# Gated mix of two attentions on one core: the first block of x loaded ahead of the first weights, which come and are cast in two halves

## The chip, the core and the metric

The kernel runs on one NeuronCore of a Trainium2 chip. The metric is the time of one execution on the device, in microseconds (us). The core has five engines that run their own instruction streams and wait for each other with semaphores: TensorE (PE; its weight loads are listed apart as PEld), VectorE (DVE), ScalarE (ACT), GpSimd (POOL) and SyncE (SP), which here issues all DMA transfers. Data come from the chip's memory (DRAM) into on-chip tiles of 128 partitions, and TensorE writes its products into PSUM banks.

## The reference

One token sequence x of 2048 tokens by 448 features goes through two attention layers of 16 heads with 28 features each, and a gate of each token mixes their outputs.

```python
g = sigmoid((x * gate_w).sum(-1, keepdims=True))
# A: linear attention; features of q and k by a small matrix of each head and two softmaxes
pq, pk = q_A @ w_phi, k_A @ w_phi
phi_q = concat(softmax(pq), softmax(-pq));  phi_k = concat(softmax(pk), softmax(-pk))
a = ((phi_q @ (phi_k.T @ v_A)) / (phi_q @ phi_k.sum(0) + 1e-6)) @ A_wo
# B: full softmax attention
b = (softmax(q_B @ k_B.T * 28 ** -0.5) @ v_B) @ B_wo
out = g * a + (1 - g) * b
```

q, k and v of each layer are x times that layer's wqkv. All inputs and the output are float32.

## The kernel before, in words

**Precision.** TensorE is fast on a rounded 32-bit type (fp32r). A float32 matrix is therefore split into a high part, its cast to fp32r, and a low part, what the cast left out. A product of two such matrices is three products: high by high, high of x by low of w, low of x by high of w. XH and XL hold the high and low parts of x, wB those of B's weights for q and k.

**Tiling.** The 448 features are four blocks b of 128 partitions; the last block holds 64 rows twice, so that its upper half can take the low part of x there (L718). The tokens are cut into four columns t of 512. Layer B's q and k come out as seven row blocks m of 128 by 512 tokens, a unit (m, t) being one PSUM bank: 11 products for a unit (3 for each of the blocks 0 to 2, 2 for the block 3).

**The start.** `first_units` (L696 to L732) makes the units m = 0 to 3 of t = 0 side by side, in four banks, while its data arrive. For each block b, SP issues two loads of 256 KB: the first 512 columns of the weights (L701) and 512 tokens of x (L702), both into the two halves of one buffer `raw[b]`. Buffers 0 to 2 are from the pool `stg`, of three; buffer 3 is from the pool `ev`. `x_loads(1)` (L703, issued at L141) asks for the next 512 tokens, into the same three buffers of `stg`, so these loads wait until a buffer has been read. Then come eight products of the identity with itself (L707, L708) into the fourth bank. Nothing reads them, and the first useful product there starts the bank anew. They are float32, which TensorE runs as two records each. The identity is made by GpSimd at the very start (masks.py:197 and 199).

For each block the casts follow: ScalarE casts the weights (L711), VectorE casts x for block 0 and ScalarE for the others (L712), VectorE subtracts for the low parts of the weights (L713) and of x (L715, L718). TensorE's products (L725) are written in this order for blocks 0 to 2: the four m with high by high, the four m with the low part of the weights, the four m with the low part of x. For block 3 it goes by m. That makes 44 products. A load of the weights of a product (PEld) stands ahead of each.

**After it.** Units 4 to 19 of B's q and k (`proj_qk`, L118) use the next x; then layer A's keys, values and queries with feature maps, B's values, and a first pass over B's scores that takes maxima (L296, L337, L348). From about 330 us on, the scores of B are computed again (L1040), go through the exponential on ScalarE (L1043) and meet the values (L1144), group by group; the two outputs are projected and mixed at the end.

**What sets the order.** The order on TensorE, VectorE, ScalarE and GpSimd is that of the program text. SP is not in that list: the framework's scheduler orders the DMA issues on it. DMAs tell of their landing by eight semaphores that are taken in turn.

The change touches `first_units` alone.

Of the kernel before, what the change touches and what calls it, by code (L numbers as in the profile page):

```python
# [17 lines left out]
P = 128  # L18
# [17 lines left out]
def f32(ap):  # L36
    return ap.bitcast(F32)
# [3 lines left out]
def gated_mix_kernel(ctx, tc, xT, wqkB, wvB, wvA, wkAT, wqAT, phi, woA, woB,  # L41
# [7 lines left out]
    nc = tc.nc  # L49
# [14 lines left out]
    def ps_s(nm):  # L64
        if turn4:
            turn4.append(nm)
            if len(turn4) % 4 == 0:
                return ps_pv(nm)
        return ps.tile([P, 512], F32, tag="s", name=nm, bufs=psn[0])

    def ps_pv(nm):
        return ps.tile([P, 512], F32, tag="pv", name=nm, bufs=1)

    def ps_mx(nm, d):
        return ps.tile([P, 2, 512], F32, tag="md" if d and psn[1] == 3 else "mx", name=nm,
                       bufs=1 if d and psn[1] == 3 else 2)
# [582 lines left out]
    def keep_qk(m, t, pq, ev):  # L659
        tt = slice(t * 512, (t + 1) * 512)  # L660
        e = ev.tile([P, 2, 512], F32R, tag="ev", name=f"ev{t}_{m}")
        nc.scalar.copy(e[:, 0, :], pq)  # L662
        nc.vector.tensor_sub(e[:, 1, :], pq, f32(e[:, 0, :]))  # L663
        nc.sync.dma_start(qk_d[m * P:(m + 1) * P, :, tt], f32(e))
# [14 lines left out]
    def x_loads(t):  # L679
        loads(("x", t), lambda: load_x(t, 0), lambda: load_x(t, 2))  # L680
# [7 lines left out]
    def splits(n):  # L688

        if n % 4 == 1 and n < 12:  # L690
            split_x(n // 4 + 1, raws.pop(("x", n // 4 + 1)))
        if n in (14, 15):
            split_part(wB[1], "wB1", 384, n - 14)
        take_lows()

    def first_units():  # L696

        raw = [stg.tile([P, 2, 512], F32, tag="stg", name=f"first_raw{b}") for b in range(3)]
        raw.append(f32(ev.tile([P, 2, 512], F32R, tag="ev", name="first_raw3")))
        for b in range(4):  # L700
            nc.sync.dma_start(raw[b][:, 0, :], wqkB[:, b, :512])  # L701
            nc.sync.dma_start(raw[b][:, 1, :], xT[:, b, :512])  # L702
        x_loads(1)  # L703
        pqs = [ps_s(f"pqk0_{m}") for m in range(3)] + [ps_pv("pqk0_3")]
        pr = [ps_mx(f"pqk_{i}", False) for i in range(2)]
        later.extend((pr[0][:, 0, :], pr[1][:, 0, :]))
        for _ in range(8):  # L707
            nc.tensor.matmul(pqs[3][:, :P], ident, ident, start=True, stop=True)  # L708
        for b in range(4):
            w, x = wB[0][:, :, b, :], XH[:, b, :512]  # L710
            nc.scalar.copy(w[:, 0, :], raw[b][:, 0, :])  # L711
            (nc.scalar.copy if b else nc.vector.tensor_copy)(x, raw[b][:, 1, :])  # L712
            nc.vector.tensor_sub(w[:, 1, :], raw[b][:, 0, :], f32(w[:, 0, :]))  # L713
            if b < 3:
                nc.vector.tensor_sub(XL[:, b, :512], raw[b][:, 1, :], f32(x))  # L715
                todo = [(0, x), (1, x), (0, XL[:, b, :512])]
            else:
                nc.vector.tensor_sub(x[64:], raw[b][64:, 1, :], f32(x[64:]))  # L718
                todo = [(0, x), (1, x)]
            if b < 3:  # L720
                order = [(i, m) for i in range(3) for m in range(4)]
            else:
                order = [(i, m) for m in range(4) for i in range(2)]
            for i, m in order:
                nc.tensor.matmul(pqs[m], w[:, todo[i][0], m * P:(m + 1) * P], todo[i][1],  # L725
                                 start=b == 0 and i == 0, stop=b == 3 and i == 1,
                                 skip_group_check=True)
        hold = raws[("x", 1)][0][:1, 0, :4]
        splits(1)
        nc.gpsimd.tensor_copy(phi_s[:1, :, 0], hold)  # L730
        for m in range(4):
            keep_qk(m, 0, pqs[m], ev)  # L732

    later = []
    first_units()
    pkv = ps_pv("pkv")
    for n in range(4, NP):
# [637 lines left out]
```

## Time and profile before

| what | us |
|---|---|
| median of 3 runs (1001.2 to 1002.0) | 1001.29 |
| the profiled execution, its time | 1001.51 |
| its span, first to last instruction | 999.7 |
| TensorE busy | 991.4 |
| ScalarE busy | 807.4 |
| VectorE busy | 666.3 |
| GpSimd busy | 231.7 |
| mean granted TensorE clock | 0.999 |

The profile is of one execution. Its times count from the first instruction, and the execution's own time is 1.8 us longer than the span. A timeline row reads: start in us, length in us, engine, line of the kernel, operation, output tile <- input tile, shapes, count (x8 means that eight neighbours were merged, and the length is that of all), and in brackets the time that the engine stood idle before it and what ended that. SPq rows are the issues of DMAs: the length is the issue's own, and the data land later. A line of the chain of waits gives start, length and what the end of the program was waiting for at that time. Records of TensorE products overlap: a new one starts before the one ahead of it has ended, so the distance of starts is what a product costs.

### The profile page before, as it was taken

How to read it: one execution, taken by the hardware profiler on the slowest of the kernel's cores; microseconds unless marked ns; L12 is line 12 of the kernel's file. 1: busy time of each engine (PE TensorE's matmuls, PEld its weight loads, DVE VectorE, ACT ScalarE, POOL GpSimd, SP SyncE). 2: the span in 40 equal slices, each digit the busy share in tenths (PEclk: the TensorE clock that was granted, in tenths of full speed). 3: DMA queues.
4: the chain of work that ended last, by engine and by line, in shares of the span. 5: the costliest groups of instructions: out<-in, count | busy, mean ns of one | idle time of the engine just before them, and what ended most of it. 6: DMA issues, size and time to landing. Idle time of an engine off the chain costs nothing.

```text
span 999.7 us, 18087 instructions
## 1 busy us (share of the span) xinstructions
PE 991.4 (99%) x6456; PEld 553.5 (55%) x6456; DVE 666.3 (67%) x1343; ACT 807.4 (81%) x1532; POOL 231.7 (23%) x214
## 2 busy tenths in 40 slices
PE   9999999999999999999999999999999999999998
PEld 8878878887777533333333333333334444455656
DVE  6567666888764588878888788888886544444202
ACT  5445555568855899999999999999999999979672
POOL 1265455668415111110120100102001011101010
PEclk9999999999999999999999999999999999999999
DMA  8976312412445732332524324443233354216231
GB/s 291 316 243 211 121 59 78 169 46 79 119 131 133 163 96 56 78 79 64 114 58 108 81 51 142 90 99 94 59 90 77 76 113 120 51 37 148 62 106 56
DMA packets 69170, 109.09 MB, mean 109 GB/s; under 512 B 18216, under 2 KB 29112, under 8 KB 69080
## 3 DMA queue, kind: packets, MB, share of 16 engines
q1 hardware_dynamic: 69080, 107.94, 40.0%
q8 instruction: 51, 0.84, 0.4%
q14 instruction: 39, 0.32, 0.1%
HBM read 74.33 MB, written 31.45 MB: 106 GB/s over the span
## 4 chain that ended last, share of the span: by engine, by line
PE 95%; DMA 2%; SPq 1%; DVE 1%; issue 1%; ACT 0%; POOL 0%; POOLq 0%; DVEq 0%; ACTq 0%
PE st L1040 28%; PE pv L1144 25%; PE pm L337 9%; PE pqk L118 6%; PE pva L136 4%; PE pk L136 4%; PE pq L118 4%; PE pob L118 3%; PE pvb L136 2%; PE poa L118 2%; PE pmb L296 2%; PE pft L558 1%; PE pqk L725 1%; PE pkv L512 1%; DMA oTa<-oTa 1%; PE poL L1182 1%
## 5 line engine op out<-in xcount | busy, mean ns | idle before, releaser
L1043 ACT ACTIVATE p<-st 128x512 f32<-128x512 f32 x1020 | 527.2, 638 | 25.9 <-PE st L1040 25.9
L348 DVE TENSOR_REDUCE part<-pm 128x1 f32<-128x512 f32 x450 | 287.3, 685 | 150.5 <-PE pm L337 150.5
L1040 PE MATMUL st<-qst,kst 128*128 128x512 f32 x1020 | 301.0, 423 | 0.4 <-DVE acc L1159 0.4
L1144 PE MATMUL pv<-p,vb 128*32 128x512 f32 x2048 | 263.7, 602 | 0.0
L1040 PEld LDWEIGHTS st<-qst,kst 128*128 128x128 f32 x1020 | 168.7, 187 | 99.6 <-ACT p L1043 45.0
L341 ACT ACTIVATE rl<-pm 128x512 f32<-128x512 f32 x200 | 124.3, 622 | 13.9 <-PE pm L337 12.4
L337 PEld LDWEIGHTS pm<-kc,qc 28*128 28x128 f32 x800 | 38.2, 181 | 167.7 <-issue 101.4
L441 POOL TENSOR_TENSOR oUb<-oUb,rsb 128x512 f32<-128x512 f32 x15 | 19.3, 1288 | 460.9 <-DMA rsb<-rdb 299.1
L345 DVE CUSTOM_DVE_ANT_0 rl<-pm,rl 128x512 f32<-128x512 f32 x150 | 102.0, 680 | 0.0
L337 PE MATMUL pm<-kc,qc 28*128 28x512 f32 x800 | 101.3, 495 | 0.0
L1144 PEld LDWEIGHTS pv<-p,vb 128*32 128x32 f32 x2048 | 47.3, 108 | 95.6 <-issue 89.5
L305 DVE CUSTOM_DVE_ANT_0 rl<-pmb,rl 128x512 f32<-128x512 f32 x112 | 72.0, 680 | 34.9 <-ACT rl L303 34.8
L303 ACT ACTIVATE rl<-pmd 128x1024 f32<-128x1024 f32 x56 | 57.5, 1027 | 17.9 <-issue 8.7
L118 PE MATMUL pqk<-XH,wB 128*128 128x512 f32 x192 | 59.3, 397 | 0.0
L662 ACT CAST ev<-pqk 128x512 fp32r<-128x512 f32 x28 | 16.0, 589 | 36.6 <-PE pqk L118 25.2
L118 PE MATMUL poa<-woA_s,oTa 128*128 128x448 f32 x128 | 38.0, 378 | 2.8 <-DMA oTa<-oTa 2.4
L118 PEld LDWEIGHTS pqk<-XH,wB 128*128 128x128 f32 x192 | 35.4, 188 | 8.5 <-issue 1.5
L1159 DVE SCALAR_TENSOR_TENSOR acc<-pob,gate,acc 128x448 f32<-128x448 f32 x12 | 8.2, 680 | 47.3 <-PE pob L118 47.3
L136 PE MATMUL pva<-wvA_s,XH 128*128 128x450 f32 x128 | 38.6, 375 | 0.0
L136 PE MATMUL pk<-wkA_s,XH 128*128 128x448 f32 x128 | 37.5, 374 | 0.0
L118 PE MATMUL pq<-wqA_s,XH 128*128 128x448 f32 x128 | 37.3, 374 | 0.0
L663 DVE TENSOR_TENSOR ev<-pqk,ev 128x512 fp32r<-128x512 f32 x28 | 19.0, 689 | 27.0 <-ACT ev L662 24.3
(169 smaller groups left out, 1172.6 us busy)
## 6 DMA issues: line engine op xcount, KB each, us to landing
qkd<-ev SPq DMA_DIRECT2D x28, 512.0 KB
qst<-qkd SPq DMA_DIRECT2D x64, 224.0 KB
kst<-qkd SPq DMA_DIRECT2D x64, 224.0 KB
od<-oTb SPq DMA_DIRECT2D x48, 112.0 KB
rsa<-rda SPq DMA_DIRECT2D x32, 128.0 KB
rsb<-rdb SPq DMA_DIRECT2D x15, 256.0 KB
kc<-qkd SPq DMA_DIRECT2D x64, 56.0 KB
gad<-ga SPq DMA_DIRECT2D x16, 224.0 KB
```

What stands on the lines that cost most here:

```text
L118: nc.tensor.matmul(d, l, r, start=i == 0, stop=i == len(todo) - 1)
L136: nc.tensor.matmul(dst[:, :n], l, r, start=i == 0, stop=i == len(todo) - 1, skip_group_check=True)
L296: nc.tensor.matmul((pb if j < 2 else pd)[:, j % 2, :], qc[js, qt * P:(qt + 1) * P], kc[js, :], start=True, stop=True, tile_position=(32 * ...
L303: nc.scalar.activation(rl, pd, AF.Relu)
L305: nc.vector.tensor_tensor_reduce(rl[:, i, :], pb[:, i, :], rl[:, i, :], 1.0, LOWEST, ALU.add, ALU.max, part[:, col + i:col + i + 1])
L337: nc.tensor.matmul(pm[j], mxs[("qc", gq)][js, qt * P:(qt + 1) * P], mxs[("kc", g, kb)][js, :], start=True, stop=True, tile_position=(32 * ...
L341: nc.scalar.activation(rl, pm[kb], AF.Relu if kb < 3 else AF.Copy)
L345: nc.vector.tensor_tensor_reduce(r, pm[j], r, 1.0, LOWEST, ALU.add, ALU.max, part[:, col + j:col + j + 1])
L348: nc.vector.tensor_reduce(part[:, col + j:col + j + 1], pm[j], AX.X, ALU.max)
L1040: nc.tensor.matmul(st, kst_of[(gq // NQ, kt // 4)][:, j, (kt % 4) * P:(kt % 4 + 1) * P], qst_of[gq][:, j, :], start=True, stop=True)
L1043: nc.scalar.activation(p, st, AF.Exp, scale=SCALE)
L1144: nc.tensor.matmul(pv[32 * j:32 * j + 32, :], vb[kt // 8][:, kt % 8, 4 * g + j, :], pt[j], start=kt == 0, stop=kt == NT - 1, tile_position ...
```

## The change

Four things change in `first_units`. The load of x's block 0 is issued first. The weights of block 0 come behind it as two loads of 256 columns each, and ScalarE casts them in two instructions of 256 columns. The blocks 1 to 3 keep their loads and casts. The banks of the four units are claimed at the top. Two of the eight warming products no longer use the identity: VectorE clears 128x128 elements of buffer 3, in the place that the fourth block's weights take later, and two products run on that; six run on the identity as before, behind the statements that issue the loads.

```diff
         raw.append(f32(ev.tile([P, 2, 512], F32R, tag="ev", name="first_raw3")))
-        for b in range(4):
+        pqs = [ps_s(f"pqk0_{m}") for m in range(3)] + [ps_pv("pqk0_3")]
+        a = raw[3][:, 0, :P]
+        nc.vector.memset(a, 0.0)
+        for _ in range(2):
+            nc.tensor.matmul(pqs[3][:, :P], a, a, start=True, stop=True)
+        nc.sync.dma_start(raw[0][:, 1, :], xT[:, 0, :512])
+        for c in (0, 256):
+            nc.sync.dma_start(raw[0][:, 0, c:c + 256], wqkB[:, 0, c:c + 256])
+        for b in range(1, 4):
             nc.sync.dma_start(raw[b][:, 0, :], wqkB[:, b, :512])
             nc.sync.dma_start(raw[b][:, 1, :], xT[:, b, :512])
         x_loads(1)
-        pqs = [ps_s(f"pqk0_{m}") for m in range(3)] + [ps_pv("pqk0_3")]
         pr = [ps_mx(f"pqk_{i}", False) for i in range(2)]
         later.extend((pr[0][:, 0, :], pr[1][:, 0, :]))
-        for _ in range(8):
+        for _ in range(6):
             nc.tensor.matmul(pqs[3][:, :P], ident, ident, start=True, stop=True)
         for b in range(4):
             w, x = wB[0][:, :, b, :], XH[:, b, :512]
-            nc.scalar.copy(w[:, 0, :], raw[b][:, 0, :])
+            for c in range(0, 512, 512 if b else 256):
+                cs = slice(c, c + (512 if b else 256))
+                nc.scalar.copy(w[:, 0, cs], raw[b][:, 0, cs])
             (nc.scalar.copy if b else nc.vector.tensor_copy)(x, raw[b][:, 1, :])
             nc.vector.tensor_sub(w[:, 1, :], raw[b][:, 0, :], f32(w[:, 0, :]))
```

## The prediction

> **What bounds the kernel now.** I read the page's busy shares first, then its chain of work that ended last.
>
> ```profile
> PE 991.4 (99%) x6456; PEld 553.5 (55%) x6456; DVE 666.3 (67%) x1343; ACT 807.4 (81%) x1532; POOL 231.7 (23%) x214
> PE 95%; DMA 2%; SPq 1%; DVE 1%; issue 1%; ACT 0%; POOL 0%; POOLq 0%; DVEq 0%; ACTq 0%
> ```
>
> TensorE works for 991.4 of 999.7 us, so whatever brings its useful work forward can be kept to the end, and only that. Next the first pieces of the chain in order of time, since the change touches nothing behind 15 us.
>
> ```profile
> 1.36 3.68 PE pqk L708 x16
> 5.04 10.04 PE pqk L725 x44
> 15.08 22.44 PE pqk L118 x99
> ```
>
> The columns are start, length, what. Warming products run to 5.04, then 44 useful ones at 10.04 / 44 = 0.228 us each, without a hole. So the term to find is how far the 44 move as a row, and which of them waits for data after the change. For that, the timeline of the first 8 us.
>
> ```profile
> 0.74 0.39 SPq L701 DMA_DIRECT2D first_raw<-in_wqkB_dram  x1
> 0.81 0.09 DVE L172 MEMSET red<- 128x32 f32 x1 [0.81 <-PEq L1362]
> 1.01 0.29 POOL masks.py:199 TENSOR_SCALAR_AFFINE_SELECT ident<-ident 128x128 f32<-128x128 f32 x1
> 1.19 0.41 SPq L702 DMA_DIRECT2D first_raw<-in_xT_dram  x1
> ...
> 1.36 3.68 PE L708 MATMUL pqk<-ident 128*128 128x128 f32 x16 [1.36 <-POOL ident masks.py:199]
> 1.65 0.43 SPq L701 DMA_DIRECT2D first_raw<-in_wqkB_dram  x1
> 2.12 0.43 SPq L702 DMA_DIRECT2D first_raw<-in_xT_dram  x1
> ...
> 3.54 0.43 SPq L701 DMA_DIRECT2D first_raw<-in_wqkB_dram  x1
> 3.63 0.62 ACT L711 CAST wB<-first_raw 128x512 fp32r<-128x512 f32 x1 [1.61 <-DMA first_raw<-in_wqkB_dram]
> ...
> 4.28 0.43 DVE L712 CAST XH<-first_raw 128x512 fp32r<-128x512 f32 x1 [3.39 <-DMA first_raw<-in_xT_dram]
> 4.63 0.68 DVE L713 TENSOR_TENSOR wB<-first_raw,wB 128x512 fp32r<-128x512 f32 x1
> 4.83 1.67 PEld L725 LDWEIGHTS pqk<-XH,wB 128*128 128x128 f32 x8
> 4.86 2.06 PE L725 MATMUL pqk<-XH,wB 128*128 128x512 f32 x8
> 5.23 0.68 DVE L715 TENSOR_TENSOR XL<-first_raw,XH 128x512 fp32r<-128x512 f32 x1
> 5.96 0.62 ACT L711 CAST wB<-first_raw 128x512 fp32r<-128x512 f32 x1 [1.71 <-DMA first_raw<-in_wqkB_dram]
> ...
> 6.64 0.62 ACT L712 CAST XH<-first_raw 128x512 fp32r<-128x512 f32 x1
> ```
>
> The first useful weight load stands at 4.83: the last input, x's cast, ends at 4.28 + 0.43 = 4.71, and 0.12 us later TensorE goes. That 0.12 is my hand-over below. But a second thing ends there as well:
>
> ```profile
> 4.51 0.33 PEld L708 LDWEIGHTS pqk<-ident 128*128 128x128 f32 x1
> ```
>
> The last warming load runs from 4.51 to 4.84. Data and warming train end together, and moving one alone brings nothing.
>
> **The change, part by part.** *Warming train.* Today it waits for the identity (GpSimd, 1.01 + 0.29 = 1.30) and starts at 1.36, 0.06 later. The new first two products need a 128x128 clear on VectorE behind the 0.09 us one at 0.81. No row shows that clear on VectorE: not below 0.09 (a quarter of the columns), not above the 0.29 of the identity's GpSimd step; I take 0.2, nearer the upper since it is the same shape. 0.90 + 0.2 + 0.06 = 1.16, so the train starts and ends about 0.18 us earlier (bounds 0.10 to 0.31). VectorE pays nothing: it idles 3.39 us before 4.28. The length stays eight products.
>
> *x first.* x takes the slot of 0.74 on SP and lands as the weights did, by 3.63; cast on VectorE 3.63 to 4.06, 0.65 earlier than now. Every later load of the queue moves one slot back, since the halves are one issue more: 1.65 to 2.12, that is 0.47. The fourth weight block's load now also waits for two warming products that read its buffer; they are done at about 2.1 (1.16 and a quarter of the train's 3.68), that load comes at 3.54 + 0.47 = 4.01, so nothing queued behind it on SP (the last x block and the x loads of L141) is held.
>
> *Weights in halves.* The rate of the transfers:
>
> ```profile
> 2.50:3.63 1.13, 1.13 (x7) 1.13 (x6) 0.00 (x0) 0.00 (x1) 0.00 (x0) 1.00 1.02 386
> 3.63:4.28 0.65, 0.65 (x5) 0.65 (x4) 0.00 (x0) 0.62 (x1) 0.00 (x0) 1.00 1.15 337
> 4.28:5.96 1.68, 1.68 (x10) 1.51 (x9) 1.63 (x3) 0.01 (x1) 0.00 (x0) 1.00 0.92 276
> ```
>
> The last two columns are the busy share of the DMA engines and GB/s. They are full from 2.5 us on, and 256 KB at 386 GB/s is 0.68, which agrees with 4.28 - 3.63 = 0.65 between the first two landings. So a transfer costs its bytes and the earlier issue of a later one hides: 0.47 of issue is less than 0.65 of transfer. At best the halves land at 3.96 and 4.28. At worst each costs what a whole block does, 0.65: 4.28 and 4.93. I take the bytes, with up to 0.1 more for twice the rows. The Trainium skill's page DMA: Bandwidth & Descriptors (Anatomy of one DMA) gives each transfer some 2 us fixed plus its bytes, which taken as a serial price would put the second half 2 us later; the 0.65 between two landings here says that this share overlaps.
>
> The cast of a half on ScalarE has a row in the tail of the kernel:
>
> ```profile
> L1243 ACT CAST oTlast<-oUlast x2: 403/404/406, 989.8 to 990.1; 128x256 fp32r<-128x256 f32 x2
> ```
>
> First half 3.96 + 0.40 = 4.36, hand-over to 4.48: data is ready 0.35 earlier than 4.83. The train is not: with 0.18 it lets the useful row go at 4.65. Second half 4.28 + 0.40 = 4.68, needed by the third product at about 5.1: covered.
>
> *Where the stall goes.* The fifth product needs the low part of the weights, and VectorE takes it from the whole 512 columns.
>
> ```profile
> 5.63 0.19 PEld L725 LDWEIGHTS pqk<-XH,wB 128*128 128x128 f32 x1
> ```
>
> Today the low part is done at 4.63 + 0.68 = 5.31, and its load at 5.63 waits for nothing. After: 4.68 + 0.03 + 0.68 = 5.39, with the hand-over 5.51, while TensorE wants it at 5.63 - 0.18 = 5.45. It waits 0.06, or 0.16 if the halves cost 0.1 more. Of 0.18, 0.02 to 0.12 is left.
>
> Then comes the second block. Its weights land at 5.96, its x is cast by 6.64 + 0.62 = 7.26.
>
> ```profile
> 7.44 1.77 PEld L725 LDWEIGHTS pqk<-XH,wB 128*128 128x128 f32 x8
> ```
>
> TensorE wants it at 7.44; with the hand-over it is there at 7.38. So at most 0.06 of the gain passes this point, as long as that block lands when it does now; with 0.1 more for the halves it is 0.04 of loss. Behind it there is cover:
>
> ```profile
> 8.26 0.62 ACT L712 CAST XH<-first_raw 128x512 fp32r<-128x512 f32 x1
> 10.16 1.77 PEld L725 LDWEIGHTS pqk<-XH,wB 128*128 128x128 f32 x8
> 12.40 1.05 ACT L377 CAST XH<-xraw 128x1024 fp32r<-128x1024 f32 x1 [0.45 <-DMA xraw<-in_xT_dram]
> 14.70 0.41 PEld L118 LDWEIGHTS pqk<-XH,wB 128*128 128x128 f32 x2
> ```
>
> The third block is cast at 8.88 and wanted at 10.16, the next x at 13.45 against 14.70. A delay of under 1.2 us is lost in there.
>
> **Sum.** Between -0.06 and +0.04 us; I take -0.05. The profiled execution took 1001.51 us, of which the span is 999.7 and 1.8 lie around it: it becomes 1001.46. It stood 0.22 above the median of the three runs, 1001.29, which therefore becomes **1001.2 us**: no change that a measurement tells. A measurement of this kernel can tell about 0.2%, 2 us, from no change; the three runs alone spread over 0.8 us.
>
> **Rivals.** *The gain is kept.* For it: landings 0.65 apart would put the second block's weights at 4.93 and not at 5.96; the 276 GB/s row shows that they were slowed, perhaps by chance. Then the second block binds nothing and 0.12 to 0.18 remain: 1001.1. Against it: it needs an accident to go away.
>
> *The extra transfer holds the second block.* If issue and not bytes set its landing, it comes 0.47 later, cast by 7.73, wanted at 7.44, there at 7.85: +0.4; with each half as dear as a whole block, 7.26 + 0.65 + 0.12 = 8.03, +0.6. 1001.7 to 1001.9. Against it: the full DMA engines from 2.5 us on.
>
> *The clock comes late.* Warming is for the TensorE clock:
>
> ```profile
> 1.36:4.86 3.50, 3.50 (x17) 3.50 (x17) 0.58 (x2) 1.27 (x2) 0.84 (x1) 1.00 0.76 242
> L708 PEld LDWEIGHTS pqk<-ident x16: 288/333/333, 1.4 to 4.5; 128*128 128x128 f32 x16
> L558 PEld LDWEIGHTS pft<-ident,feat x128: 137/140/143, 190.0 to 264.1; 128*128 128x128 f32 x128
> ```
>
> The clock column says 1.00 for the train, but the same load of 128x128 takes 333 ns there and 140 ns later: the train ran at about half speed, and the first useful load at 4.83 takes 0.19 as all later ones do. So the clock doubled near 4.8, about 3.4 us after TensorE began. I count on it to move with the train. If it does not, each us of delay makes TensorE do half of what it could: half of the delay is lost, at most half of another 3.4, 1.7 us: up to 1003.0, if the doubling fell one such stretch later. The Trainium skill's page TensorE: Matmul & The Clock Gate (Part 1) says just this, that the window of 3413 ns runs free and does not start with the kernel. The 3.4 us here agree with its length; one trace can't show its phase, and by that rule the kernel before has the same lottery.
>
> *The order on SP flips, and it is slower.* Only the four compute engines have their order written by hand; SP's is made by the scheduler:
>
> ```profile
> 11.54 0.42 SPq L749 DMA_DIRECT2D sel_s<-in_sel_dram  x1
> 13.24 2.10 SPq L141 DMA_DIRECT2D xraw<-in_xT_dram  x2
> ```
>
> L749 is written at unit 14 and goes ahead of x loads written at unit 5. One more DMA at the head could change an order later. The place where that costs is the stretch where TensorE waits for a chain of DMAs:
>
> ```profile
> 279.75 3.57 DMA oTa<-oTa
> ...
> 300.71 3.55 DMA oTa<-oTa
> ```
>
> One issue slipped behind such a landing costs 3.6 us: 1004.9. It decides from the point where an issue of these chains stands behind one that it precedes now. Against it: the plan shifts as a whole, by less than one slot of 0.47 us. The same slip the other way would save up to 3.6: 997.7.
>
> **How the numbers follow.** Forecast 0.50; gain kept 0.13; second block held 0.17; late clock 0.10; SP order slower 0.06, faster 0.04. Faster by over 0.2% (under 999.3) is the last alone, 0.04; slower (over 1003.3) the one before, 0.06; within 0.2%: 0.90. The range takes in the first three cases, 0.80, the runs' own spread, and a late clock of up to half its price: 1000.5 to 1002.4.
>
> **What the profile after would show.** The train from about 1.16; the first useful load at about 4.65 (at 4.5 if the train is not what holds it, at 4.8 if the halves land late); a short hole ahead of the fifth product, with VectorE's low part named; the second block's first load at 7.38 to 7.48; from 15 us on the same picture, shifted by less than 0.1. Wrong it would be if that second load stands past 7.8, if useful products ahead of some later point are 0.45 us apart (the clock), or if the stretch from 255 to 304 us changes its length.

## The result, and the profile after

The changed kernel takes 1003.48 us (median of 10 runs, 1001.37 to 1005.51), the kernel before 1001.60 in the runs beside it (10 runs, 1001.2 to 1002.1). The ratio is 1.0018, with a 95% interval of 1.0009 to 1.0026. That is a loss of 1.9 us where 0.05 of gain was forecast, and the time lies above the forecast's range of 1000.5 to 1002.4. The profiled execution of after took 1005.02 us with a span of 1003.2, 3.5 more than that of before.

The page's busy shares and its chain by engine:

```profile
PE 993.7 (99%) x6456; PEld 555.6 (55%) x6456; DVE 666.8 (66%) x1344; ACT 806.9 (80%) x1533; POOL 232.5 (23%) x214
PE 88%; DMA 6%; SPq 2%; DVE 2%; POOL 1%; issue 1%; ACT 1%; POOLq 0%; ACTq 0%; DVEq 0%
```

TensorE is as full as before, but its share of the chain fell from 95% to 88%, and DMA took up 4 of the 7 points. So somewhere DMAs now set the end. First the start of the kernel, from the timeline of after:

```profile
0.74 0.40 SPq L705 DMA_DIRECT2D first_raw<-in_xT_dram  x1
...
1.09 1.22 PE L704 MATMUL pqk<-first_raw 128*128 128x128 f32 x4 [1.09 <-DVE first_raw L702]
...
3.67 0.43 DVE L721 CAST XH<-first_raw 128x512 fp32r<-128x512 f32 x1 [2.64 <-DMA first_raw<-in_xT_dram]
...
3.99 0.40 ACT L720 CAST wB<-first_raw 128x256 fp32r<-128x256 f32 x1 [1.98 <-DMA first_raw<-in_wqkB_dram]
4.53 1.20 PE L734 MATMUL pqk<-XH,wB 128*128 128x512 f32 x2
...
5.61 0.41 ACT L720 CAST wB<-first_raw 128x256 fp32r<-128x256 f32 x1 [1.21 <-DMA first_raw<-in_wqkB_dram]
6.04 0.69 DVE L722 TENSOR_TENSOR wB<-first_raw,wB 128x512 fp32r<-128x512 f32 x1 [1.94 <-ACT wB L720]
6.06 1.94 PE L734 MATMUL pqk<-XH,wB 128*128 128x512 f32 x6 [0.33 <-ACT wB L720]
...
7.12 0.62 ACT L720 CAST wB<-first_raw 128x512 fp32r<-128x512 f32 x1 [1.10 <-DMA first_raw<-in_wqkB_dram]
7.41 3.41 SPq L141 DMA_DIRECT2D xraw<-in_xT_dram  x3
```

Everything up to the first useful product went as planned: it starts at 4.53, 0.33 ahead of before. Then the **second half of the weights** is cast only at 5.61, when ScalarE had idled 1.21 us for its DMA; the first half was cast at 3.99, so the halves landed 1.6 us apart. TensorE has two products to do meanwhile, which fill 1.20 us at the half clock of the start, and it still idles 0.33. Block 1's weights come at 7.12 instead of 5.96, and the first load of the next x (L141), which waits for buffer 0 to be read, is issued at 7.41 instead of 5.98, where before has it:

```profile
5.98 0.39 SPq L141 DMA_DIRECT2D xraw<-in_xT_dram  x1
```

What DMA did in that time, in windows of 0.5 us (the last three columns are granted clock, busy share of the DMA engines and GB/s). Before:

```profile
3.50:4.00 0.50, 0.50 (x4) 0.50 (x4) 0.00 (x0) 0.37 (x1) 0.00 (x0) 1.00 0.98 336
4.00:4.50 0.50, 0.50 (x4) 0.50 (x3) 0.22 (x1) 0.25 (x1) 0.00 (x0) 1.00 1.05 283
4.50:5.00 0.50, 0.50 (x5) 0.50 (x4) 0.50 (x2) 0.00 (x0) 0.00 (x0) 1.00 0.95 217
```

After:

```profile
3.50:4.00 0.50, 0.50 (x4) 0.50 (x4) 0.33 (x1) 0.01 (x1) 0.00 (x0) 1.00 0.71 121
4.00:4.50 0.50, 0.50 (x5) 0.50 (x4) 0.10 (x1) 0.39 (x1) 0.00 (x0) 1.00 0.47 152
4.50:5.00 0.50, 0.50 (x3) 0.50 (x3) 0.00 (x0) 0.00 (x0) 0.00 (x0) 1.00 1.01 287
```

From 3.5 to 4.5 us the DMA engines moved less than half of what they moved before, and they were idle for part of it (shares 0.71 and 0.47), though more loads had been issued. The forecast had read "full from 2.5 us on" off the trace of before and carried it over to another list of transfers.

The thin stretch is not the whole of the late landing, though. The trace also has each row that the DMA engines moved, and the two halves are 256 rows of 1 KB. Of these, 242 had begun by 4.5 us; the last 14 began between 4.5 and 5.19, while the engines already moved mostly the next block, at 287 and 328 GB/s. The 16 semaphore updates by which the second half tells of its landing come from 3.75 to 5.58 us. So a few rows hold back the landing of the whole; why they lag is open.

How the delay came to the end is read from the chain of after up to 64 us:

```profile
9.15 5.03 DMA xraw<-in_xT_dram
...
20.26 6.77 DMA qkd<-ev
...
36.72 7.35 DMA qkd<-ev
...
48.04 6.78 DMA wvA_raw<-in_wvA_dram
...
60.90 1.30 POOL kp L230
62.27 1.27 POOL kp L230
63.58 0.49 PE pmd L296
```

Before, this stretch was TensorE alone (5.04, then 15.08 in the chain that the prediction shows). Now the late x is waited for, then transfers of q and k (each some 7 us from issue to landing), the weights of A's values, GpSimd's casts of them and its subtraction at 60.90, on which TensorE waits for 0.61 us, until 63.58. The third place is at 283 us, where TensorE waits for `oTa`. From windows over 3.5 us of after, with the same columns (ahead of the clock stand the busy time and count of each engine, PE first):

```profile
282.20:285.77 3.57, 1.83 (x11) 1.16 (x10) 3.12 (x7) 2.21 (x5) 0.01 (x1) 1.00 0.50 153
285.77:289.20 3.43, 3.42 (x9) 3.09 (x10) 1.82 (x5) 0.43 (x1) 1.34 (x3) 0.50 0.28 110
```

and the same work in before:

```profile
279.80:283.40 3.60, 2.33 (x14) 1.59 (x12) 2.63 (x7) 2.24 (x4) 0.00 (x0) 1.00 0.38 110
283.45:286.90 3.45, 3.45 (x20) 2.92 (x20) 2.27 (x5) 1.50 (x3) 1.37 (x3) 1.00 0.25 98
```

In the stretch with that wait TensorE was busy for 1.83 us here and for 2.33 in before; behind the wait its granted clock is 0.50 for 3.4 us in after, and it gets 9 products done where before did 20.

So the profiled 3.5 us are a sum of places. I took the start of the same TensorE product in both traces and subtracted: after is 1.11 us late at 15 us, 1.78 at 63, 2.33 at 283, 3.9 behind the half clock, 3.54 at the end. Between 63 and 265 us it stays at 1.78 to 1.84, so most of what came in up to 283 us (0.43 of 0.55) came in at the wait for `oTa` itself.

### The profile page after: what moved, and what is told of

Its sections match the earlier page's. It is cut to its first block, busy times and chain, and to the rows that moved or that the text cites. A ratio compares the mean times of both kernels' runs of the same rounds, so it can differ in the third digit from the quotient of the medians.

```text
span 1003.2 us, 18092 instructions
## 1 busy us (share of the span) xinstructions
PE 993.7 (99%) x6456; PEld 555.6 (55%) x6456; DVE 666.8 (66%) x1344; ACT 806.9 (80%) x1533; POOL 232.5 (23%) x214
## 4 chain that ended last, share of the span: by engine, by line
PE 88%; DMA 6%; SPq 2%; DVE 2%; POOL 1%; issue 1%; ACT 1%; POOLq 0%; ACTq 0%; DVEq 0%
PE st L1049 28%; PE pv L1153 25%; PE pm L337 9%; PE pva L136 4%; PE pk L136 4%; PE pq L118 3%; PE pob L118 3%; PE pvb L136 2%; DMA qkd<-ev 2%; PE pqk L118 2%; PE poa L118 2%; PE pmb L296 2%; PE pft L558 1%; SPq L461 1%; PE pkv L512 1%
```

## The experiments

Each kernel was timed against the kernel before on the same chip. Where an expectation names a theory by a letter: C is that the new warming delays the doubling of the clock; P, that a place in the queue is slow, whatever transfer stands in it; H, that the halved casts cost (in the section on the half clock H is another one, that the wait for `oTa` makes the clock halve); D, that the late release of buffer 0, and with it the late x, carries the delay on; S, in the first four runs, that a half costs as much as a whole block, and from f1 on, that each extra transfer holds those behind it by 0.6 to 0.9 us; B, that bytes set the price and a late landing is chance. Against D stands that the delay of the start is simply kept.

Two numbers of each trace are used throughout: when the clock doubles (the trace's record of the granted clock begins there; ahead of it products take twice as long), and when the first x load of L141 is issued. "At 15", "at 63" and "end" are the offsets against the profile of before, as above. They are of one profiled execution each, and these are not all typical: those of after (1005.02), e2 (1004.34) and f1 (1004.49) were among the slowest of their kernels, that of g2 (1001.85) was the fastest. The time is the median of 10 or 11 runs, with the median of before beside it.

| kernel | clock doubles | x load | at 15 | at 63 | end | time | before | ratio, interval |
|---|---|---|---|---|---|---|---|---|
| before | 4.80 | 5.98 | 0 | 0 | 0 | | | |
| after | 5.87 | 7.41 | 1.11 | 1.78 | 3.54 | 1003.48 | 1001.60 | 1.0018 (1.0009 to 1.0026) |
| e1_x_first_whole | 5.90 | 6.27 | 0.60 | 0.17 | 0.15 | 1001.54 | 1002.11 | 0.9992 (0.9983 to 1.0001) |
| e2_halves_old_order | 6.17 | 6.16 | 0.75 | 1.04 | 2.90 | 1002.23 | 1002.11 | 1.0004 (0.9995 to 1.0013) |
| e3_clear_only | 7.15 | 5.83 | 1.01 | 0.58 | 0.20 | 1001.25 | 1002.11 | 0.9992 (0.9983 to 1.0001) |
| e4_loads_only | 4.21 | 7.08 | 0.74 | 1.30 | 1.47 | 1002.91 | 1002.11 | 1.0007 (0.9998 to 1.0016) |
| f1_after_again | 6.11 | 6.81 | 1.18 | 3.16 | 3.01 | 1003.23 | 1002.08 | 1.0014 (1.0005 to 1.0023) |
| f2_whole_load_half_casts | 5.52 | 6.59 | 0.41 | 0.62 | 0.34 | 1001.73 | 1002.08 | 0.9995 (0.9986 to 1.0004) |
| f3_tiny_load | 7.44 | 6.14 | 1.39 | 1.19 | 1.37 | 1002.70 | 1002.08 | 1.0007 (0.9998 to 1.0016) |
| f4_own_buffer | 4.99 | 5.13 | 1.12 | 0.69 | 0.74 | 1002.29 | 1002.08 | 1.0007 (0.9998 to 1.0016) |
| g1_before_own_buffer | 6.58 | 4.5 | 0.80 | 0.37 | 0.10 | 1001.74 | 1001.74 | 0.9997 (0.9988 to 1.0006) |
| g2_after_fill | 4.47 | 7.31 | 0.98 | 0.55 | 0.40 | 1003.21 | 1001.74 | 1.0013 (1.0004 to 1.0022) |
| g3_clear_own_buffer | 5.61 | 4.5 | 0.39 | -0.04 | -0.60 | 1001.14 | 1001.74 | 0.9993 (0.9984 to 1.0002) |
| g4_clear_own_fill | 4.64 | 4.5 | -0.14 | -0.46 | -0.26 | 1001.91 | 1001.74 | 0.9998 (0.9989 to 1.0007) |
| h1_three_tiny | 7.14 | 6.0 | 1.08 | 1.41 | 1.50 | 1003.06 | 1001.57 | 1.0015 (1.0006 to 1.0025) |
| h2_four_rows | 4.76 | 5.8 | -0.04 | 0.73 | 0.57 | 1002.63 | 1001.57 | 1.0009 (0.9999 to 1.0018) |

### The parts of the change

**x first, weights whole**: the changed kernel with block 0's weights in one load and one cast.

```diff
-        for c in (0, 256):
-            nc.sync.dma_start(raw[0][:, 0, c:c + 256], wqkB[:, 0, c:c + 256])
+        nc.sync.dma_start(raw[0][:, 0, :], wqkB[:, 0, :512])
...
-            for c in range(0, 512, 512 if b else 256):
...
+            nc.scalar.copy(w[:, 0, :], raw[b][:, 0, :])
```

> The changed kernel, but block 0's weights in one load and one cast; x first and the cleared tile stay. Theory P (place): the third transfer on the queue meets a few slow DMA engines at about 4 to 5.5 us whatever it carries; here the third is block 1's weights as in the kernel before, which has slack to 7.4 us, so the time is within 0.5 us of before and the casts of block 0 both start by 4.4 us. Theory S (size): a half costs as much as a whole transfer; no halves here, so also within 0.5 us of before. Theory C (clock): the altered warming moves the doubling of the clock and later dips; then this run is as slow as the changed kernel, 1.5 to 2 us over before.

Measured: 1001.54, 0.57 under before; the interval of the ratio reaches to 1.0001. The loss is gone with the halves; x first and the warming on a cleared tile don't cost in this kernel. One thing more differs from after, which the edit doesn't show: the scheduler issues two other loads earlier here, `sel_s` at 4.50 us (12.31 in after) and `mask_s` at 11.97 (17.20).

**Halves in the old order**: before, with the weights of block 0 as two loads and two casts ahead of x.

```diff
...
-        for b in range(4):
+        for c in (0, 256):
+            nc.sync.dma_start(raw[0][:, 0, c:c + 256], wqkB[:, 0, c:c + 256])
+        nc.sync.dma_start(raw[0][:, 1, :], xT[:, 0, :512])
+        for b in range(1, 4):
...
```

> The kernel before, but block 0's weights in two loads and two casts, ahead of x as before; warming as before. Theory P: the third transfer is x's block 0; it lands at 5.3 to 5.9 us instead of 4.28, so the first product stands at 5.8 to 6.3 us instead of 4.86, and the time is 1 to 2 us over before, while the second half lands by 4.3. Theory S: the second half itself is late, its cast starts at 4.9 us or later, and x behind it. Theory C: no change, warming is untouched.

Measured: 1002.23, ratio 1.0004, no difference shown. Its timeline:

```profile
2.84 0.40 ACT L716 CAST wB<-first_raw 128x256 fp32r<-128x256 f32 x1 [0.83 <-DMA first_raw<-in_wqkB_dram]
3.57 0.40 ACT L716 CAST wB<-first_raw 128x256 fp32r<-128x256 f32 x1 [0.32 <-DMA first_raw<-in_wqkB_dram]
...
4.46 0.43 DVE L717 CAST XH<-first_raw 128x512 fp32r<-128x512 f32 x1 [3.56 <-DMA first_raw<-in_xT_dram]
```

Here the halves come at 2.84 and 3.57, and the transfer behind them, the third of the queue, is cast at 4.46. In after the third place is the second half, cast at 5.61. So theory P falls: the third place isn't slow as such. Theory S, which wanted the second half's cast at 4.9 or later, falls here too. What was late in after is what had not landed by about 4.5 us.

**The clear alone**: before with the warming of after; the loads and casts as they were.

```diff
+        a = raw[3][:, 0, :P]
+        nc.vector.memset(a, 0.0)
+        for _ in range(2):
+            nc.tensor.matmul(pqs[3][:, :P], a, a, start=True, stop=True)
...
-        for _ in range(8):
+        for _ in range(6):
```

> The kernel before with only the warming changed: two of eight products on the cleared tile; loads and casts as before. Theories P and S: within 0.4 us of before. Theory C: the whole loss is here, 1.5 to 2 us over before, with runs whose clock is 0.998.

Measured: 1001.25, 0.86 under before, not slower. Theory C falls: in its profile the clock doubled as late as 7.15, and yet the end is only 0.20 late.

**The loads alone**: after with the eight old warming products and no clear.

```diff
-        a = raw[3][:, 0, :P]
-        nc.vector.memset(a, 0.0)
-        for _ in range(2):
-            nc.tensor.matmul(pqs[3][:, :P], a, a, start=True, stop=True)
...
-        for _ in range(6):
+        for _ in range(8):
```

> The changed kernel with the warming of before: x first and halves, eight products on the identity. Theories P and S: as slow as the changed kernel, 1.5 to 2 us over before, with the second half's cast at about 5.6 us in the profile. Theory C: within 0.5 us of before.

Measured: 1002.91, 0.80 over before, with an interval of the ratio that just takes in 1 (0.9998). Its timeline has the same late second half:

```profile
4.01 0.40 ACT L716 CAST wB<-first_raw 128x256 fp32r<-128x256 f32 x1 [1.99 <-DMA first_raw<-in_wqkB_dram]
...
5.27 0.40 ACT L716 CAST wB<-first_raw 128x256 fp32r<-128x256 f32 x1 [0.86 <-DMA first_raw<-in_wqkB_dram]
```

Against e1, in the same series and without halves, it is 1.37 slower. So the loss comes with the halves behind x, without the clear.

### The load or the casts, the delay or what follows it

**After again**, with no edit, to have it on the same chip as the next three.

> The changed kernel once more, beside the three that follow. Theory S (each transfer of 128 rows takes 0.6 to 0.9 us of the queue, whatever its bytes, so the second half lands at 5 to 5.6 us) and the rival B (bytes, with a chance hiccup near 4 to 5.5 us) both: 0.8 to 2 us over before.

Measured: 1003.23, 1.15 over before. The second half was cast at 5.01 in this profile, so the delay of that landing varies, but not to nothing.

**One load, two casts**: after with the whole load, the halved casts kept.

```diff
-        for c in (0, 256):
-            nc.sync.dma_start(raw[0][:, 0, c:c + 256], wqkB[:, 0, c:c + 256])
+        nc.sync.dma_start(raw[0][:, 0, :], wqkB[:, 0, :512])
```

> The changed kernel with block 0's weights in one load, still cast in two halves. Theory S: the cost is that of the extra transfer, so it is gone: weights land by 4.3 us, second cast done by 5.1, time 1 to 2 us below the changed kernel, within 0.6 of before or faster. A rival H (the cost is in the two casts and the low part that waits for both): no better than the changed kernel. Rival B: between, since the hiccup may hit any transfer behind 4 us.

Measured: 1001.73 (1000.95 to 1002.12), against 1003.23 (1002.01 to 1004.55) of after: the loss is gone. Its timeline:

```profile
4.49 0.71 ACT L719 CAST wB<-first_raw 128x256 fp32r<-128x256 f32 x2 [2.48 <-DMA first_raw<-in_wqkB_dram]
4.95 2.37 PE L733 MATMUL pqk<-XH,wB 128*128 128x512 f32 x8
...
6.59 0.38 SPq L141 DMA_DIRECT2D xraw<-in_xT_dram  x1
```

Both casts run back to back from 4.49, and the eight products follow without a hole. Theory H falls. DMA was thin here too:

```profile
3.50:4.00 0.50, 0.50 (x4) 0.50 (x4) 0.11 (x1) 0.00 (x0) 0.00 (x0) 1.00 0.80 221
4.00:4.50 0.50, 0.50 (x5) 0.50 (x3) 0.31 (x1) 0.01 (x1) 0.00 (x0) 1.00 0.58 201
```

Yet the whole load had landed by 4.49, so the thin stretch alone doesn't make the late landing. The loss goes with the second transfer. As in e1, though, `sel_s` goes ahead of the next x (4.51) and `mask_s` is earlier (11.84). No run has whole weights behind x with the issue order of after, so whether these two loads help further on is untested; block 0 has landed before they are issued.

**A tiny load**: before, with 128 rows of 16 elements (8 KB), which nothing reads, loaded behind x's block 0.

```diff
             nc.sync.dma_start(raw[b][:, 1, :], xT[:, b, :512])
+            if b == 0:
+                nc.sync.dma_start(z_s, xT[:, 0, :16])
```

> The kernel before with one more load on the queue, of 128 rows of 64 bytes, behind the two of block 0 (its tile is overwritten later, nothing reads it). Theory S: 8 KB cost a place of 0.6 to 0.9 us: block 1's weights land at 6.4 to 7 us instead of 5.9, the first load of the next x is untouched by that (it waits for buffer 0), time 0.2 to 0.8 us over before. Rival B: 8 KB are 0.02 us, nothing moves.

Measured: 1002.70, 0.62 over before; the ratio's interval takes in 1. In its timeline block 1's weights are cast at 7.58, where before has 5.96:

```profile
7.58 0.62 ACT L713 CAST wB<-first_raw 128x512 fp32r<-128x512 f32 x1 [3.19 <-DMA first_raw<-in_wqkB_dram]
```

8 KB can't do that by their bytes: 256 KB took 0.65 in before. Theory S had 6.4 to 7 for that landing, so 7.56 is beyond it. Of the 16 semaphore updates of that landing 15 had come by 6.23 us, and the last came at 7.56: one part came late, and neither h1 nor h2 below repeats that. Rival B, by which nothing moves, missed it as well.

**A buffer of its own for the next x**: after, with the first tile of the next x in the pool `ev`, so that its load doesn't wait for buffer 0.

```diff
-        raw = stg.tile([P, 2, 512], F32, tag="stg", name=nm)
+        raw = (f32(ev.tile([P, 2, 512], F32R, tag="ev", name=nm)) if nm == "xraw1_0"
+               else stg.tile([P, 2, 512], F32, tag="stg", name=nm))
```

> The changed kernel, but the first load of the next x has a buffer of its own and needn't wait until block 0's is read. Theory D: most of the loss comes from that wait, since the late half holds the low parts on VectorE, these hold buffer 0, and the loads of x behind it shift the DMA-bound stretch up to 62 us; here that load issues by 5.1 us instead of 7.1 to 7.4, and the time falls by 0.8 to 1.5 us below the changed kernel. Rival K: TensorE's own 0.7 to 1.0 us at the start is what is kept to the end; then the time stays within 0.4 us of the changed kernel.

Measured: 1002.29, 0.94 less than after, 0.21 over before; neither difference is clear of the runs' spread, so the times alone don't tell. Its chain of waits at the start:

```profile
5.65 0.41 ACT wB L721
6.06 0.04 issue
6.10 10.10 PE pqk L735 x42
16.20 22.44 PE pqk L118 x99
```

The second half is as late as in after (cast at 5.65), and the offset at 15 us is the same 1.12. But from 6.10 on the chain is TensorE again, with no DMA in it, and the offset goes down to 0.69 at 63 us instead of up to 1.78. So in this execution nothing of the start's delay grows on the way, as theory D has it; that the start's offset is kept whole falls. That the buffer is the reason is not shown by one profile: g2 below has no such buffer, its next x is issued at 7.31, and its fastest execution has no DMA in the chain either.

**The same buffer in before**, as a control.

> Control for the run with a buffer of its own: the kernel before with that buffer. Theory D (the release of buffer 0 matters because it comes late after the change): here the load issues at 4.5 instead of 6.0, which no stage of the kernel before needs, so the time stays within 0.4 us of before. Rival E (an earlier load helps any version): 0.7 to 1 us below before, and then the run with the buffer told nothing of the change.

Measured: 1001.74 on both sides. In before the buffer brings nothing, so the smaller loss of f4 is not a gain that the buffer makes in any kernel.

### The half clock at 285 us

**After, with the wait filled**: eight products that nothing reads ahead of the eleventh output tile of A (t = 10), to keep TensorE busy while it waits for `oTa`.

```diff
+        if t == 10:
+            for _ in range(8):
+                nc.tensor.matmul(po[:, :P], ident, ident, start=True, stop=True)
```

> The changed kernel with eight products of the identity into the bank of the eleventh output tile, ahead of that tile's own products, which overwrite them; they fill TensorE's wait of 1.8 to 2.3 us near 283 us. Theory H (that wait makes the clock halve for 3.4 us in some executions, 1.5 to 1.7 us each): no execution shows a clock of 0.998, the highest time falls to 1004 or less, the median by 0.2 to 0.5 against the changed kernel. Rival: the clock halves for another reason; 0.998 stays in two to three of eleven executions.

Measured: 1003.21 (1001.85 to 1004.92), so no gain in the median, and the highest time is above the 1004 that theory H gave. No execution shows 0.998. In its timeline the wait is filled:

```profile
282.14 2.05 PE L636 MATMUL poa<-ident 128*128 128x128 f32 x16
283.94 0.66 PE L118 MATMUL poa<-woA_s,oTa 128*128 128x448 f32 x2
```

**The clear alone, with the own buffer**, and **that with the wait filled**, as a better version and its control.

> The kernel before with the cleared tile for two warming products and the buffer of its own, loads and casts as before: what is left of the change if the halves and the turned order are left out. Expected 0.5 to 1.2 us below before (the cleared tile alone gave 0.9 below); by rival E 1.5 below.

> The last one with the filling products near 283 us as well. Theory H: no clock of 0.998, the time 0 to 0.3 us below the run without filling, highest time nearer to the median. If the filling ends after the data come, up to 0.3 above.

Measured: 1001.14 without the filling and 1001.91 with it: the filling itself costs 0.77. By that much g2's gain, if it has one, is hidden. A mean granted clock of 0.998 marks the executions with a half clock. It stands in 3 of 10 of after (1005.02, 1005.28 and 1005.51; the other seven lie from 1001.37 to 1003.79), and over all kernels with an extra transfer and no filling in 12 of 85 (f4 3, e2 and h2 2 each, f1 and f3 1 each, e4 and h1 none). Before has 6 of 118 in the four series of experiments, the five unfilled kernels without an extra transfer none of 55, the two with the filling none of 22. So it comes more often with an extra transfer, and the filling fits with its absence; but of the two filled kernels only g2 has an extra transfer, and its 11 runs are too few to call the wait the cause. The trace shows what it costs where it comes: some 1.5 us (the offset goes from 2.33 to 3.9 in after, from 1.43 to 2.99 in e2).

The traces also show when it comes. In all sixteen, whenever the clock falls, at 285 us or at the very end of the program, it falls a whole number of 3.413 us steps after it doubled (82 steps, 279.89 us, in after and in e2). If such steps are counted from the doubling on, TensorE is busy for 1.68 us in the step ahead of the fall at 285 us in after and for 1.59 in e2. Of the steps that end within the program, each with under 1.7 us busy is followed by a fall, and none with more is; the next ones up are 1.82 in h1 and 1.91 in f4. So what fits all sixteen is that the clock halves behind a step that is less than about half busy, and where the steps lie goes with the doubling at the start: e1 has a stretch of 3.41 us with only 1.69 busy, but it straddles two steps. Only two of the falls are at 285 us, and no run moved the wait against the steps by intent.

### What one more transfer costs

**Three tiny loads** in the place of the one, and **one of four rows**.

```diff
+            if b == 0:
+                for d in (z_s, gate, gate1):
+                    nc.sync.dma_start(d, xT[:, 0, :16])
```

> The kernel before with three more loads of 128 rows of 64 bytes behind block 0's two (into tiles that are overwritten later). Theory S, a place per transfer: block 1's weights, at 7.56 us with one such load, come 0.9 to 1.5 us later still, at 8.4 to 9.1; TensorE waits for them; time 1.2 us or more over before. Rival B (chance hiccup, the one load had bad luck): at 6 to 7.6 us, time as with one load or less.

```diff
+            if b == 0:
+                nc.sync.dma_start(z_s[:4], xT[:4, 0, :16])
```

> As with one tiny load, but of 4 rows of 64 bytes instead of 128. If the place is the price of the rows, block 1's weights come as in the kernel before, 5.8 to 6.3 us, and the time is within 0.4 us of before. If it is the price of a transfer as such (its issue on SP, 0.46 us), they come at 6.4 us or later and the time is 0.3 us or more over before.

Measured: 1003.06 (1.49 over before, interval 1.0006 to 1.0025) and 1002.63 (1.06 over, interval 0.9999 to 1.0018, its runs in two clumps: five from 1001.5 to 1002.2, five from 1003.1 to 1003.8). Block 1's weights, three tiny loads ahead:

```profile
6.30 0.62 ACT L714 CAST wB<-first_raw 128x512 fp32r<-128x512 f32 x1 [2.06 <-DMA first_raw<-in_wqkB_dram]
```

and four rows ahead:

```profile
6.14 0.62 ACT L713 CAST wB<-first_raw 128x512 fp32r<-128x512 f32 x1 [2.02 <-DMA first_raw<-in_wqkB_dram]
```

Theory S wanted 8.4 or later for three. It falls: the three landed at 4.42, 4.63 and 4.80, 0.2 apart, and the next block is 0.3 later than in before. Rival B had the landing right (6 to 7.6) and the time wrong, for the kernel is 1.5 us slower. With four rows the landing is as in before, yet the time is over the 0.4 that went with it; its interval takes in 1, as that of the one tiny load does. So three extra transfers do cost; for one tiny load it is not shown, and e2, with one more as well, shows no difference. It is not by way of that landing. Two other ways stand untested: every load behind the three is issued 1.4 us later (the last block load at 5.44 instead of 4.02), and each extra transfer moves those behind it to another of the eight semaphores.

## Why the prediction was wrong, point by point

- **The train, x, the first half: right.** The train started at 1.09 (1.16 forecast; the clear took 0.17, not 0.2), x was cast at 3.67 (3.63), the first half at 3.99 (3.96), and the first useful product stood at 4.53, the 4.5 given for a train that doesn't hold it.
- **"A transfer costs its bytes": the step that failed.** The second half was forecast to land at 4.28 to 4.38, at worst 4.93, and was called covered for the third product, wanted at about 5.1. That product started at 6.06 in after, behind 0.33 of idle time. The half was cast at 5.61, 5.27, 5.01, 5.65 and 5.51 in the five profiles with halves behind x: later than the worst bound each time. The bound was the distance of two landings between 3.6 and 4.3 us in before, while the DMA engines were full; the very next rows of before had them move 283 and 217 GB/s, and its block 1 landed 1.68 us behind x. I had read that row and called it "perhaps by chance". In every profile the first block or half of a block that had not landed by about 4.5 us came late (block 1's weights at 5.7 to 6.4 in nine kernels and in before, where block 0 comes whole or its halves come first; 7.6 in f3). The change pushed half of block 0, which everything waits for, into that time. There the last rows decide and not the bytes: in after 242 of the halves' 256 rows had begun by 4.5 us.
- **"The extra transfer holds the second block"** was the rival of the right kind: priced at +0.4 to +0.6 at that block, with its weights 0.47 to 0.65 later. They were 1.16 later (7.12), the first weight load of that block's products stood at 8.53, past the 7.8 that the prediction named as a sign of being wrong, and what it set off was not in the price.
- **"Behind it there is cover; a delay of under 1.2 us is lost in there": failed too.** I followed the data of the products up to 15 us. I did not follow the buffer that the late step releases, whose next load went out at 7.41 instead of 5.98, nor how little slack the DMAs behind it have up to 55 us. Six profiles have DMAs in the chain between 7 and 55 us (after, f1, e4, e2, f2, h2), and there the offset grows from 15 to 63 us, by 0.67, 1.98, 0.56, 0.29, 0.21 and 0.77. The other nine kernels with edits have TensorE alone there, all four with the own buffer among them, and in eight of them it falls by 0.20 to 0.43 (in h1 it grows by 0.33). So in those six what the slack swallowed came back through DMA. The time of the first x load alone doesn't sort the two groups, though: g2, at 7.31, has no DMA in its chain, and h2, at 5.8, has. Nor does the kernel: after, f1 and g2 have the same start, and in g2's fastest execution nothing came back (0.40 at the end). Which transfer tips it over stays open.
- **The late clock: the rival was right in mechanism, and right that half of the delay is lost; "I count on it to move with the train" was not.** The train of after started 0.27 us earlier than that of before, and its clock doubled 1.07 later. The clock doubled 2.85 to 6.08 us after TensorE's first product, in no order with the edits, and where block 0's weights come whole the offset at 15 us is about half of the clock's delay: (7.15 - 4.80) / 2 = 1.18 against 1.01 in e3, 0.55 against 0.60 in e1, 0.36 against 0.41 in f2, 0.89 against 0.80 in g1. With halves behind x, 0.5 to 1.2 stand on top: after 1.11 against 0.54, e4 0.74 against -0.30, f4 1.12 against 0.10. The Trainium skill's page TensorE: Matmul & The Clock Gate (Part 1) has the window run free of the kernel, and these traces agree. What I missed is that the profile of before, with 4.80, was itself one of the earlier draws, the fifth of sixteen, so that each offset against it holds a piece that no edit made.
- **"The order on SP flips": not in after.** There the issues kept their order; it flipped in e1 and f2, where `sel_s` and `mask_s` came earlier, at no loss. The place near 283 us was touched in another way: the wait for `oTa` near 283 us was followed by a half clock of 3.4 us in the profiled run, at some 1.5 us. The Trainium skill's page TensorE: Matmul & The Clock Gate (Part 1) has the clock fall back behind a whole idle window of about 3.4 us; here it fell behind 3.57 us of which TensorE was busy for 1.83. So the measurement differs from that rule: a step that was half idle was enough.
- **A fixed price of each transfer in series: rightly set aside.** The prediction weighed the fixed 2 us of each transfer (the Trainium skill's DMA: Bandwidth & Descriptors, Anatomy of one DMA) as a price in series and took it to overlap. That section measures it for transfers that GpSimd issues; here SyncE issues them. Three tiny loads landed 0.2 us apart, each 2.2 to 2.8 us after its issue, so what is fixed does overlap.

**What is shown, what is open.** Shown: the loss comes with the load that is split behind x (e1, f2, e3 without, e4 with), the clear doesn't make it, nor do the casts; the second half lands late in all five profiles with halves behind x, and TensorE loses 0.5 to 1.2 us at the start by it; in six of the seven profiles whose offset grows from 15 to 63 us the chain goes through DMA there, and in none of the eight where it shrinks. Of after's 1.9 us the seven runs at full clock show 1.4. Argued, not shown: that a buffer of its own for the next x keeps DMA out of the chain (f4, with g1 as control, but g2 against it). Open: which transfer tips the chain over to DMA; how much of e1's and f2's recovery behind the start comes from their other issue order; why DMA is thin there with loads waiting, and why the last rows of a transfer lag; by which way three tiny loads, which hardly move the next landing, cost 1.5 us; and why 0.43 us came in at the wait for `oTa`. The clear alone (e3 -0.86, g3 -0.60) beats the changed kernel; against before its intervals reach to 1.0001 and 1.0002, so a gain is likely and not shown.

## What to carry to other kernels

Splitting a load to start sooner helps only if the second piece lands where the first would have let the work go on; read the landings that follow in the trace of before, and price the piece by the slowest of them, not by the best. If a scheduler orders the issues, compare the whole list of issues before two runs are called one edit apart. A delay that the data's slack swallows can come out again further on. A buffer that is released late is one possible way: follow the release to the next load, and that load to its first reader. Where a clock steps up by itself, compare traces behind that step only after its own half delay is taken off.

## What was not expected of the hardware

- DMA engines idle with loads issued: busy shares of 0.71 and 0.47 at 121 and 152 GB/s between 3.5 and 4.5 us, between stretches at 215 or more.
- The landing of one and the same 128 KB varied from 5.0 to 5.65 us over five profiles. Its 16 semaphore updates come from 3.75 to 5.58 us in after; in f3 one late update holds a block of 256 KB for 1.3 us.
- The granted clock falls to 0.50 for 3.4 us after a stretch in which TensorE was about half busy (1.83 of 3.57 us), late in the kernel and not in each execution. In sixteen traces each fall comes a whole number of 3.413 us steps after the doubling, behind a step with under 1.7 us busy.
- Eight products of 128x128 in float32 put into a wait of TensorE cost 0.77 us of the whole time (1001.91 against 1001.14).
